# Numerators of two query pairs and transposed rows of the last pair copied to SBUF by ScalarE, and split from there with GpSimd

## The chip, the cores and the metric

One core of a Trainium2 chip runs the whole kernel. The metric is the device time of one execution in microseconds (us). The kernel before takes 561.29 us, the median of 3 runs (561.02 to 561.9).

## What is computed

Two linear-attention blocks work on the same rows x (2048 rows of 576), with 32 heads of 18, and a gate mixes their results row by row. Cut to what matters here:

```python
g = _sigmoid((x * gate_w).sum(-1, keepdims=True))
# block a: phi = where(t > 0, t + 1, exp(t)) + 1e-6
# block b: phi = [softmax(t @ w_phi), softmax(-(t @ w_phi))]
kv  = jnp.einsum("bhsd,bhse->bhde", phi(k), v)
z   = phi(k).sum over s
num = jnp.einsum("bhqd,bhde->bhqe", phi(q), kv)
den = jnp.einsum("bhqd,bhd->bhq", phi(q), z)[..., None] + 1e-6
return g * (num_a / den_a) @ wo_a + (1 - g) * (num_b / den_b) @ wo_b
```

## The kernel before, in words

The 2048 rows are 16 tiles of 128, worked in 8 pairs. Three stages follow each other: keys and values of block a, keys and values of block b, then queries and output of both. Matmul operands are kept as two parts that sum to the float32 value: a high part (F32R, a rounded copy) and a low part (value minus high part). Making both is called a split: ScalarE (A in the code, ACT in the profile) copies the value to the high part, and another engine subtracts it from the value.

This change is in the query stage, from about 290 us to the end. Its loop (lines 1285 to 1309) has nine rounds i. In round i, three strands are merged into one program:

- `q_units` (line 1163) projects pair i+1 with a Strassen product (line 500): seven products in three PSUM tiles of name `pq`, called X, Y and Z here. There are two `pq` buffers: X holds one for the whole pair, and Z takes the buffer of Y. So Z's first matmul (`pq<-tail,x`, with the lhs tile x_3670 for pair 2) waits until VectorE (V, DVE) has added Y into `row` (`row<-row,pq`, line 521). X is accumulated four times, and each time ACT first copies what it holds (`row<-pq`).
- `tr_units` (line 1193) transposes pair i on TensorE, one tile of rows after the other: four transposes of block a's normalized queries (`tr<-ident,row`), whose result in PSUM is split into `at` (high by ACT, low by DVE), and eleven of block b's (`tr<-ident,late`), which ACT copies to `uT`.
- `num` and `out_units` (lines 1214 and 1238) finish pair i-1. `num` multiplies `uT` by `kb` (which merges blocks, `tr<-uT,kb` and `bk<-uT,kb`) into two PSUM tiles `tr` and one `bk`. They are split into `vo` (high by ACT, low by DVE, lines 1227 to 1235: 128x512 for each `tr` tile, 128x256 and 64x256 for `bk`). `out_units` multiplies `at` and `vo` by the output weights: 27 matmuls for each half row, as high times high, high times low and low times high.

There are two PSUM buffers of each name (`tr`, `bk`, `pq`). A transposition into `tr` waits until both readers of the tile that was there before are through.

`norm_a` and `norm_b` (lines 1122 and 1142) divide the queries by their denominators, with work on DVE, GpSimd (G, POOL) and ACT: products with `z_a` and `z_b`, sums over heads (`dd`, `den`), reciprocals, and the scaled rows in `row` and `late`. `softmax_exp` (line 676) makes block b's exponentials in `uw`: maxima and minima (`mm`), two subtractions (`uw<-uw,mm`, `uw<-mm,uw`), one exponential on ACT, sums (`ss`).

The order on each engine is not that of the code. Every operation is recorded in a `Plan` (line 146) with a cost, a time by which it is due, and its dependencies; `run` (line 271) lists the operations by a model of the five engines, and `emit` (line 346) writes them in that order. All instructions therefore have line 354. What the model thought of durations matters on the chip only as the order that it fixed: each engine takes its instructions strictly in that order.

`wk` holds a tile `st` of 128x2x576 with one buffer (line 596). Before this change it is used last in the stage before the queries.

Of the kernel before, what the change touches and what calls it, by code (L numbers as in the profile page):

```python
# [12 lines left out]
F32 = mybir.dt.float32  # L13
F32R = mybir.dt.float32r
AF = mybir.ActivationFunctionType
ALU = mybir.AluOpType
AX = mybir.AxisListType

P = 128
S, D, H, DH = 2048, 576, 32, 18  # L20
NT = S // P
# [337 lines left out]
def tile_gated_mix(ctx, tc, xT, wAk, wAv, wBv, wAq, wkT, wqT, phi, woA, woB, out):  # L359
    nc = tc.nc  # L360
    plan = Plan()
    V, A, G, PE, SP = [Engine(plan, k, x) for k, x in (("DVE", nc.vector), ("ACT", nc.scalar), ("POOL", nc.gpsimd),
                                                       ("PE", nc.tensor), ("SP", nc.sync))]
# [3 lines left out]
    wk = Pool(plan, "wk", ctx.enter_context(tc.tile_pool(name="wk", bufs=2)), 2)  # L367
# [4 lines left out]
    def r(ap):  # L372
        return ap.bitcast(F32)
# [4 lines left out]
    def pq_tile():  # L378
        return ps.tile([P, 2, 512], F32, name="pq")

    def tr_tile():
        return ps.tile([P, 512], F32, name="tr")
# [12 lines left out]
    def bank_tile():  # L395
        return ps.tile([P, 512], F32, name="bk")
# [4 lines left out]
    def uw_tile():  # L401
        return wk.tile([P, 2, D], F32, name="uw")
# [7 lines left out]
    def at_tile(shape, dt=F32):  # L410
        return wk.tile([P] + shape, dt, name="at")

    def wide_tile(i, shape, dt=F32):
        return wk.tile([P] + shape, dt, name=("uT", "late")[i], bufs=1)
# [50 lines left out]
    def chunks(ap):  # L465
        return ap.rearrange("p (j n) -> p j n", n=P)

    def split(src, hi, lo, eng):
        A.activation(hi, src, AF.Copy)
        eng.tensor_tensor(lo, src, r(hi), op=ALU.subtract)  # L470
# [44 lines left out]
    def x_fetch(n):  # L515

        x, ts, stored = x_tiles()
        x["dma"] = []
        for t, d in zip((*ts, *stored), (*X_d[n], *S_d[n])):
            SP.dma_start(r(t), d)  # L520
            x["dma"].append(len(plan.ops) - 1)
        return x
# [245 lines left out]
    raw = area[0][:, :1280].rearrange("p (a c) -> p a c", a=2)  # L768
# [301 lines left out]
    def load_out(k, at):  # L1070
        t = op_tile() if k < 4 else tail_tile()
        WOt[k] = t
        plan.first = at
        if k < 3:
            SP.dma_start(r(t).rearrange("p (i s) n -> p i s n", i=2), WO_d[:, 2 * k:2 * k + 2])
        elif k == 3:
            to = r(t).rearrange("p (i s) n -> p i s n", i=2)
            SP.dma_start(to[:126], MA_d[:252].rearrange("(g p) s n -> p g s n", g=2))
            SP.dma_start(to[126:], MA_d[570:574].rearrange("(g p) s n -> p g s n", g=2))
        else:  # L1080
            SP.dma_start(r(t[:126]), MA_d[252:378])
            SP.dma_start(r(t[126:]), MA_d[574:])
# [80 lines left out]
    def q_units(n, x, uws, c1_tile, then={}):  # L1163
        t1, t2 = 2 * n, 2 * n + 1
        qa, qb = {}, {}

        def c11(c):
            qb[t1] = softmax_exp(c, uws[0], G)

        def c22(c, Z):  # L1170
            V.tensor_tensor(c, c, Z[:, :, :HB], op=ALU.add)
            qa[t2] = phi_elu(c)

        def c21(X):
            qb[t2] = softmax_exp(whole(X, uws[1]), uws[1])

        def c12(c, Z):
            V.tensor_tensor(c, c, Z[:, :, :HB], op=ALU.add)
            qa[t1] = phi_elu(c)

        def norm(t):
            ub = UBS[t % 2]
            qs[t] = (norm_a(t, qa[t], ub), ub)
            norm_b(t, *qb[t], ub, (G, V, G if t < 4 else V))

        x_tile = (two_banks, lambda: two_banks(bank_tile))[n] if n < 2 else pq_tile
        for i, _ in enumerate(strassen(x, WQ, TQ, HB, x_tile, c1_tile, c11, c22, c21, c12)):
            if i in then:
                then[i]()
            yield  # L1190
        norms.extend([lambda: norm(t2), lambda: norm(t1)])

    def tr_units(t, at, uT):
        f, ub = qs.pop(t)
        ath, atl = at
        c = slice(P * (t % 2), P * (t % 2) + P)

        p1 = tr_tile()
        for j in range(4):
            lo = P * j if j < 3 else 448  # L1200
            PE.transpose(p1[:, P * j:P * j + P], f[:, lo:lo + P], ident)
        src = chunks(p1)
        A.activation(ath[:, 0:4, c], src, AF.Copy)
        V.tensor_tensor(atl[:, 0:4, c], src, r(ath[:, 0:4, c]), op=ALU.subtract)
        yield
        for q in range(3):
            p1 = tr_tile()
            nb = min(4, NB - 4 * q)
            for i in range(nb):
                PE.transpose(p1[:UB, P * i:P * i + P], ub[:, UB * (4 * q + i):UB * (4 * q + i) + UB], ident)  # L1210
            A.activation(uT[:UB, 4 * q:4 * q + nb, c], p1[:UB, :P * nb].rearrange("p (j n) -> p j n", n=P), AF.Copy)
            yield

    def num(uT, at, last):
        ath, atl = at
        oh, ol = ot = [wk.tile([P, KT, 256], F32R, name="vo") for _ in range(2)]
        if last:
            q = pq_tile()
            pms = [q[:, 0], q[:, 1], tr_tile()]
        else:  # L1220
            pms = [tr_tile(), tr_tile(), bank_tile()]
        with plan.piece():
            for b in range(NB):
                a, k = b % 2, b // 2 % 2
                PE.matmul(pms[b // 4][64 * a:64 * a + 64, 256 * k:256 * k + 256], kb[:, b, :], uT[:UB, b, :], start=True, stop=True,
                          skip_group_check=True)
        for m, p1 in enumerate(pms):
            j = 2 * m
            n = 2 if j < 4 else 1
            src = p1[:, :256 * n].rearrange("p (j n) -> p j n", n=256)  # L1230
            A.activation(oh[:, j:j + n], src, AF.Copy)
            V.tensor_tensor(ol[:, j:j + n], src, r(oh[:, j:j + n]), op=ALU.subtract)
            if n == 1:
                A.activation(ath[:64, 3], p1[:64, 256:], AF.Copy)
                V.tensor_tensor(atl[:64, 3], p1[:64, 256:], r(ath[:64, 3]), op=ALU.subtract)
        return ot

    def out_units(t, blk):
        ath, atl = blk["at"]
        oh, ol = blk["ot"]  # L1240
        c = slice(P * (t % 2), P * (t % 2) + P)
        osb = row_tile()[:, :D]
        dst = out[P * at_row(t):P * at_row(t) + P]
        for hf in range(2):
            po = bank_tile()
            cc = slice(HB * hf, HB * hf + HB)
            srcs = [(ath, atl, m, 6 + m) for m in range(3)] + [(oh, ol, j, j) for j in range(KT)] + [(ath, atl, 3, 5)]
            st = []
            for hi, lo, j, i in srcs:
                st += [(hi[:, j, c], WO(0, i)), (hi[:, j, c], WO(1, i)), (lo[:, j, c], WO(0, i))]  # L1250
            for i, (l, w) in enumerate(st):
                PE.matmul(po[:, :HB], l, w[:, cc], start=(i == 0), stop=(i == len(st) - 1))
            A.activation(osb[:, cc], po[:, :HB], AF.Copy)
            if t >= NT - 2:
                SP.dma_start(dst[:, cc], osb[:, cc])
            if hf == 0:
                yield
        if t < NT - 2:
            SP.dma_start(dst, osb)
        yield  # L1260
# [10 lines left out]
    def chain(*gens):  # L1271
        for g in gens:
            yield from g
# [3 lines left out]
    uT = wide_tile(0, [NB, 256])  # L1277
# [7 lines left out]
    for i in range(NT // 2 + 1):  # L1285
        while norms:
            norms.pop(0)()
        cur, prev = blocks[i], blocks[i - 1]
        seqs = []
        if i and i <= NT // 2:  # L1290
            prev["ot"] = num(uT, prev["at"], i >= NT // 2 - 1)
        if i + 1 < NT // 2:
            x = x_fetch(pairs[i + 1])
            if i == 0:
                load_out(3, x["dma"])
                load_out(4, x["dma"])
            if i == 1:
                for k, m in enumerate((1, 4, 6)):
                    load_out(k, x["dma"][m:m + 1])
            uws = [extra_uw if i == 0 else uw_tile(), uw_tile()]  # L1300
            seqs.append((7, .7, q_units(i + 1, x, uws, row_tile)))
        ts = (2 * i + 1, 2 * i)
        if i < NT // 2:
            at = at_tile([2, 4, 256], F32R)
            cur["at"] = (at[:, 0], at[:, 1])
            seqs.append((8, 1, chain(*[tr_units(t, cur["at"], uT) for t in ts])))
        if i:
            seqs.append((4, 1, chain(*[out_units(t, prev) for t in (2 * i - 1, 2 * i - 2)])))
        merge(*seqs)
# [82 lines left out]
```

## Time and profile before

| | us |
|---|---|
| median of 3 runs | 561.29 |
| the profiled execution | 562.4 |
| its span, first to last instruction | 560.7 |
| PE (TensorE) busy | 551.6 |
| DVE busy | 421.8 |
| ACT busy | 288.3 |
| POOL busy | 245.8 |

The profile shows one execution. PE is the matmul side of TensorE and PEld its weight loads, which overlap; both are nearly always busy. Times of the timeline count from the span's start. A row of the timeline has the start, the duration, the engine, the operation with out<-in and shapes, how many alike follow each other, and in brackets how long the engine sat idle ahead of it and what ended that. The granted TensorE clock was full for the whole span.

### The profile page before, as it was taken

What the parts mean: (1) busy time and instruction counts of PE and PEld (TensorE: products, weight loads), DVE (VectorE), ACT (ScalarE), POOL (GpSimd) and SP (SyncE); (2) the same over time, 40 slices, a digit from 0 to 9 for tenths busy, and PEclk for the clock granted to TensorE, in tenths of its full rate; (3) what the DMA queues carried; (4) which work ended last, traced back from release to release, by engine and by line L of the source; (5) the groups of instructions that cost most, each with busy time, mean ns of one, the idle gap of its engine ahead of it and who ended that gap; (6) DMA issues with size and microseconds to landing.
All of it is one profiled execution on the core that took longest, in us unless ns stands there. A gap on an engine that the chain in (4) does not pass through costs nothing.

```text
span 560.7 us, 11695 instructions
## 1 busy us (share of the span) xinstructions
PE 551.6 (98%) x4584; PEld 527.7 (94%) x4584; DVE 421.8 (75%) x673; ACT 288.3 (51%) x602; POOL 245.8 (44%) x218
## 2 busy tenths in 40 slices
PE   8999999999999999999999989999999999999997
PEld 8999999999999978999998989898999989899897
DVE  5872678843897997899889998769597795978810
ACT  6666687655645544543355645435443544535421
POOL 6575487632793523363228764214152332424200
PEclk9999999999999999999999999999999999999999
DMA  8739767976759566757759622132322314100001
GB/s 282 272 116 312 252 236 253 338 245 269 273 208 384 184 214 210 250 184 261 284 182 311 247 80 77 48 105 70 106 78 85 97 44 122 51 1 23 31 34 43
DMA packets 38625, 96.22 MB, mean 172 GB/s; under 512 B 4198, under 2 KB 7782, under 8 KB 37034
## 3 DMA queue, kind: packets, MB, share of 16 engines
q1 hardware_dynamic: 38570, 95.47, 50.2%
q8 instruction: 36, 0.59, 0.4%
q14 instruction: 19, 0.16, 0.1%
HBM read 59.64 MB, written 36.70 MB: 172 GB/s over the span
## 4 chain that ended last, share of the span: by engine, by line
PE 83%; DVE 10%; POOL 2%; ACT 2%; issue 1%; DMA 1%; SPq 0%; POOLq 0%; DVEq 0%; ACTq 0%
PE pq L354 35%; PE tr L354 25%; PE bk L354 23%; DVE row L354 3%; DVE dd L354 2%; DVE den L354 1%; DVE mm L354 1%; DVE ss L354 1%; POOL late L354 1%; POOL row L354 1%; DVE at L354 1%; DMA at<-xT 1%; DVE rs L354 1%; ACT row L354 1%; ACT uw L354 0%
## 5 line engine op out<-in xcount | busy, mean ns | idle before, releaser
L354 PE MATMUL pq<-op,x 128*128 128x288 f32 (+1 forms) x636 | 102.6, 297 | 0.0
L354 PEld LDWEIGHTS pq<-op,x 128*128 128x128 f32 x636 | 90.4, 189 | 0.9 <-issue 0.4
L354 PE MATMUL bk<-op,vo 128*128 128x288 f32 x480 | 71.0, 297 | 0.0
L354 PE MATMUL pq<-tail,x 128*128 128x288 f32 (+1 forms) x308 | 66.9, 300 | 0.0
L354 PEld LDWEIGHTS bk<-op,vo 128*128 128x128 f32 x480 | 65.8, 188 | 0.2 <-DVE vo L354 0.2
L354 PE MATMUL pq<-op,xp 128*128 128x288 f32 (+1 forms) x336 | 54.0, 297 | 0.0
L354 PE MATMUL bk<-op,at 128*128 128x288 f32 x288 | 51.3, 301 | 0.0
L354 POOL TENSOR_TENSOR row<-row,z_a 128x576 f32<-128x576 f32 x16 | 22.9, 1429 | 63.3 <-issue 35.7
L354 PEld LDWEIGHTS pq<-tail,x 128*128 128x128 f32 x308 | 49.1, 188 | 1.3 <-issue 0.6
L354 ACT ACTIVATE row<-bk 128x288 f32<-128x288 f32 x38 | 15.6, 411 | 64.4 <-PE bk L354 64.4
L354 PEld LDWEIGHTS pq<-op,xp 128*128 128x128 f32 x336 | 47.5, 188 | 0.2
L354 ACT ACTIVATE row<-row,epsc 128x576 f32<-128x576 f32 x54 | 41.9, 777 | 10.5 <-DVE row L354 9.4
L354 POOL TENSOR_TENSOR row<-row,den 128x378 f32<-128x378 f32 (+1 forms) x32 | 24.6, 789 | 47.8 <-DVE den L354 39.4
L354 DVE TENSOR_REDUCE ss<-uw 128x64 f32<-128x1152 f32 x23 | 31.0, 1350 | 18.5 <-ACT uw L354 17.9
L354 ACT ACTIVATE row<-tr 128x288 f32<-128x288 f32 (+1 forms) x74 | 30.2, 409 | 28.1 <-PE tr L354 27.2
L354 PEld LDWEIGHTS bk<-op,at 128*128 128x128 f32 x288 | 41.7, 189 | 0.4 <-issue 0.4
L354 ACT ACTIVATE uw<-uw 128x1152 f32<-128x1152 f32 x23 | 26.8, 1166 | 23.8 <-DVE uw L354 13.6
L354 POOL TENSOR_TENSOR x<-at,x 128x384 fp32r<-128x384 f32 (+2 forms) x35 | 31.3, 898 | 16.5 <-ACT x L354 14.4
L354 DVE TENSOR_TENSOR row<-row,pq 128x576 f32<-128x576 f32 (+1 forms) x30 | 22.5, 750 | 18.7 <-ACT row L354 14.3
L354 PE MATMUL tr<-op,xv 128*128 128x288 f32 (+1 forms) x204 | 33.7, 302 | 0.0
L354 ACT ACTIVATE uT<-tr 118x512 f32<-118x512 f32 (+1 forms) x48 | 25.9, 559 | 14.6 <-PE tr L354 14.5
L354 DVE TENSOR_TENSOR vo<-row,pq 128x540 f32<-128x540 f32 (+1 forms) x56 | 22.8, 449 | 11.4 <-ACT row L354 10.4
(206 smaller groups left out, 1264.3 us busy)
## 6 DMA issues: line engine op xcount, KB each, us to landing
xp<-s0x SPq DMA_DIRECT2D x12, 512.0 KB
at<-xT SPq DMA_DIRECT2D x18, 320.0 KB
x<-x1x SPq DMA_DIRECT2D x12, 384.0 KB
x<-s2x SPq DMA_DIRECT2D x12, 384.0 KB
s0x<-xp SPq DMA_DIRECT2D x8, 512.0 KB
out<-row SPq DMA_DIRECT2D x14, 288.0 KB
op<-wb SPq DMA_DIRECT2D x3, 1152.0 KB
wod<-op SPq DMA_DIRECT2D x3, 1152.0 KB
```

Source lines behind the costliest of these rows:

```text
L354: fn(*[a.real() if isinstance(a, View) else a for a in args], **{k: v.real() if isinstance(v, View) else v for k, v in kw.items()})
```

## The change

In `num`, for rounds 1 and 2 (the numerators of pairs 0 and 1), each `tr` tile is copied whole to the SBUF tile `st` by ACT. The split then reads `st`: ACT makes the high part from it, and POOL the low part. The `bk` tile is split as before. In `tr_units` the same is done with the four transposes of block a for the last two row tiles (t = 15 and 14, in round 7). Six 128x512 subtractions leave DVE for POOL, and six ACT copies are new.

```diff
@@ tr_units
         src = chunks(p1)
-        A.activation(ath[:, 0:4, c], src, AF.Copy)
-        V.tensor_tensor(atl[:, 0:4, c], src, r(ath[:, 0:4, c]), op=ALU.subtract)
+        if t >= NT - 2:
+            to = chunks(raw_tile()[:, :512])
+            A.activation(to, src, AF.Copy)
+            split(to, ath[:, 0:4, c], atl[:, 0:4, c], G)
+        else:
+            A.activation(ath[:, 0:4, c], src, AF.Copy)
+            V.tensor_tensor(atl[:, 0:4, c], src, r(ath[:, 0:4, c]), op=ALU.subtract)
@@ num
+    def raw_tile():
+        return wk.tile([P, 2, D], F32, name="st", bufs=1).rearrange("p a b -> p (a b)")
+
-    def num(uT, at, last):
+    def num(uT, at, last, raw):
...
+            if raw is not None and n == 2:
+                to = raw[:, 512 * m:512 * m + 512].rearrange("p (j n) -> p j n", n=256)
+                A.activation(to, src, AF.Copy)
+                split(to, oh[:, j:j + n], ol[:, j:j + n], G)
+                continue
@@ the loop
-            prev["ot"] = num(uT, prev["at"], i >= NT // 2 - 1)
+            prev["ot"] = num(uT, prev["at"], i >= NT // 2 - 1, raw_tile() if i in (1, 2) else None)
```

The planner answers with another order of the instructions. It differs in rounds 0 to 2 and from round 7 on; between them each engine has the rows that it had.

The first place is PE in round 1, from the numerators of pair 0 on (`tr<-uT,kb`). The rows `pq<-op,xp` are X and Z of pair 2, and `pq<-tail,x_3670` opens Z. Before:

```order
L354 MATMUL tr<-uT,kb 64x256 x8
L354 MATMUL bk<-uT,kb 64x256 x3
L354 MATMUL pq<-tail,x_3718 128x288
L354 MATMUL pq<-op,xp 128x288 x6
L354 MATMUL bk<-op,vo 128x288 x2
L354 MATMUL pq<-op,xp 128x288 x6
L354 MATMUL pq<-tail,x_3670 128x288 x2
L354 MATMUL pq<-op,xp 128x288 x6
L354 MATMUL pq<-tail,x_3670 128x288 x2
L354 MATMUL pq<-op,xp 128x288 x6
L354 MATMUL pq<-op,x_3895 128x288 x12
L354 MATMUL tr<-ident,row 128x128 x4
```

With the change, PE has at the same place:

```order
L354 MATMUL tr<-uT,kb 64x256 x8
L354 MATMUL bk<-uT,kb 64x256 x3
L354 MATMUL pq<-tail,x_3718 128x288
L354 MATMUL pq<-op,xp 128x288 x6
L354 MATMUL tr<-ident,row 128x128 x4
L354 MATMUL pq<-op,xp 128x288
L354 MATMUL bk<-op,vo 128x288 x2
L354 MATMUL pq<-op,xp 128x288 x5
L354 MATMUL pq<-tail,x_3670 128x288 x2
L354 MATMUL pq<-op,xp 128x288 x6
L354 MATMUL pq<-tail,x_3670 128x288 x2
L354 MATMUL pq<-op,xp 128x288 x6
```

The four transposes have moved up, ahead of Z, and the rest is behind them.

DVE at the same time, before. The row `row<-row,pq` adds Y of pair 2, which Z waits for; `uw` are block b's subtractions for pair 1:

```order
L354 TENSOR_TENSOR row<-vo,z_b 128x576
L354 TENSOR_REDUCE dd<-row 128x32
L354 TENSOR_TENSOR row<-row,pq 128x576
L354 TENSOR_TENSOR dd<-dd,rs 128x64
L354 SCALAR_TENSOR_TENSOR den<-dd 128x32
L354 RECIPROCAL den<-den 128x32
L354 SCALAR_TENSOR_TENSOR rs<-den,gate,rs 128x64
L354 TENSOR_TENSOR uw<-mm,uw 128x576
L354 TENSOR_TENSOR at<-bk,at 64x256
L354 TENSOR_REDUCE mm<-row 128x32 x2
L354 TENSOR_TENSOR uw<-uw,mm 128x576
L354 TENSOR_TENSOR vo<-tr,vo 128x512 x2
```

And with the change:

```order
L354 TENSOR_TENSOR row<-vo,z_b 128x576
L354 TENSOR_REDUCE dd<-row 128x32
L354 TENSOR_REDUCE mm<-uw 128x32
L354 TENSOR_TENSOR uw<-mm,uw 128x576
L354 TENSOR_REDUCE dd<-row 128x32
L354 TENSOR_TENSOR dd<-dd,rs 128x64
L354 SCALAR_TENSOR_TENSOR den<-dd 128x32
L354 RECIPROCAL den<-den 128x32
L354 SCALAR_TENSOR_TENSOR rs<-den,gate,rs 128x64
L354 TENSOR_TENSOR uw<-uw,mm 128x576
L354 TENSOR_TENSOR row<-row,pq 128x576
L354 TENSOR_TENSOR at<-bk,at 64x256
```

The addition of Y has moved behind both `uw` subtractions and the chain from `dd` to `rs`, and the two `vo<-tr,vo` are gone. POOL takes them in this order after the change: `late<-vo,rs` three times, `vo<-st,vo`, `row<-uw,z_b`, `vo<-st,vo`.

The second place is ACT in round 1, late, around the exponential of pair 2 (`uw<-uw`). Before:

```order
L354 ACTIVATE at<-tr 128x4x128
L354 ACTIVATE row<-bk 128x288
L354 ACTIVATE uw<-uw 128x1152
L354 ACTIVATE row<-row 128x3x2
L354 ACTIVATE late<-row 128x10x10
L354 ACTIVATE late<-row 128x46
L354 ACTIVATE uT<-tr 118x4x128 x2
L354 ACTIVATE row<-row,epsc 128x576 x2
```

With the change:

```order
L354 ACTIVATE at<-tr 128x4x128
L354 ACTIVATE row<-bk 128x288
L354 ACTIVATE uT<-tr 118x4x128 x2
L354 ACTIVATE row<-row 128x3x2
L354 ACTIVATE row<-row,epsc 128x576
L354 ACTIVATE uw<-uw 128x1152
L354 ACTIVATE row<-row,epsc 128x576
```

The exponential has moved behind the copies of the next eight transposes (`uT<-tr`).

The third place is PE in round 7, from the numerators of pair 6 on, before:

```order
L354 MATMUL tr<-uT,kb 64x256 x3
L354 MATMUL bk<-op,at 128x288
L354 MATMUL bk<-tail,at 128x288 x3
L354 MATMUL tr<-ident,late 118x128 x3
L354 MATMUL bk<-op,vo 128x288 x2
L354 MATMUL tr<-ident,late 118x128
L354 MATMUL bk<-op,at 128x288 x3
L354 MATMUL bk<-op,vo 128x288 x13
```

With the change:

```order
L354 MATMUL tr<-uT,kb 64x256 x3
L354 MATMUL bk<-op,at 128x288
L354 MATMUL bk<-tail,at 128x288 x3
L354 MATMUL bk<-op,at 128x288 x3
L354 MATMUL bk<-op,vo 128x288 x2
L354 MATMUL tr<-ident,late 118x128 x4
L354 MATMUL bk<-op,vo 128x288 x13
```

The four transposes now stand together, behind two matmuls with the high part of `vo`; the thirteen that follow begin with its low part.

## The prediction

> **What bounds the kernel now.** I read the page's engine totals first, then TensorE's own waits, then the places of those waits in the timeline.
>
> ```profile
> PE 551.6 (98%) x4584; PEld 527.7 (94%) x4584; DVE 421.8 (75%) x673; ACT 288.3 (51%) x602; POOL 245.8 (44%) x218
> ```
>
> TensorE is busy for 551.6 of 560.7 us, and the change leaves its instructions as they are. All that it can win is idle time of TensorE, 9.1 us in all, and it can lose by making new idle time. So I asked who TensorE waits for:
>
> ```profile
> PE tr L354 <- DVE vo L354: 1.8, 2, 1.1
> ...
> PE tr L354 <- POOL late L354: 1.0, 2, 0.6
> PE tr L354 <- DVE at L354: 0.8, 1, 0.8
> ```
>
> Columns: us in total, times, longest. In the query stage these are (timeline of PE):
>
> ```profile
> 326.38 0.66 PE L354 MATMUL tr<-ident,row 128*128 128x128 f32 x4 [1.13 <-DVE vo L354]
> ...
> 335.25 1.09 PE L354 MATMUL tr<-ident,late 128*118 128x128 f32 x8 [0.33 <-POOL late L354]
> ...
> 353.97 0.63 PE L354 MATMUL tr<-ident,row 128*128 128x128 f32 x4 [0.67 <-DVE vo L354]
> 523.78 0.54 PE L354 MATMUL tr<-ident,late 128*118 128x128 f32 x3 [0.82 <-DVE at L354]
> ```
>
> Three of the four are transposes that wait for a `tr` buffer until DVE has taken the low part out of it: 1.13, 0.67 and 0.82 us, at exactly the three places that the change edits. Everywhere else in the stage TensorE is full. Why the first two occur where they do is seen in the windows (sums of busy time by engine; columns PE, PEld, DVE, ACT, POOL):
>
> ```profile
> 320.00:330.00 10.00, 8.87 (x68) 8.60 (x67) 9.66 (x18) 4.99 (x11) 7.65 (x8) 1.00 0.39 118
> ...
> 390.00:400.00 10.00, 10.00 (x78) 10.00 (x78) 6.74 (x14) 3.72 (x8) 3.90 (x4) 1.00 0.27 70
> ```
>
> In the first pairs DVE is the busy one (9.66 of 10) and POOL has 7.65; later DVE has room (6.74) and the same buffers come free in time.
>
> **The change, part by part.** What one split costs, by engine (busy us, mean ns of one):
>
> ```profile
> L354 ACT ACTIVATE vo<-tr 128x512 fp32r<-128x512 f32 x12 | 7.0, 595 | 9.3 <-PE tr L354 9.3
> L354 ACT ACTIVATE xp<-at 128x512 fp32r<-128x512 f32 x8 | 5.0, 631 | 5.7 <-PE pq L354 4.8 <-issue 0.9
> L354 DVE TENSOR_TENSOR vo<-tr,vo 128x512 fp32r<-128x512 f32 x12 | 7.6, 677 | 0.2 <-POOL late L354 0.2
> L354 POOL TENSOR_TENSOR xp<-at,xp 128x512 fp32r<-128x512 f32 x8 | 11.9, 1489 | 5.9 <-PE tr L354 3.3 <-ACT xp L354 2.6
> ```
>
> Six times, ACT gets a copy more (about 0.60), DVE loses 0.68 and POOL gains 1.49. ACT's 3.6 us lie in idle time (4.99 busy of 10 in the tightest window), and the buffer is free after one ACT copy. So the three waits fall, 1.13 + 0.67 + 0.82 us, and I also drop the 0.33 for POOL, since TensorE will arrive there later (below): **2.95 us removed.** The six copies' tile `st` has no other reader left, and the last pair's second copy comes a whole row tile after the first. No DMA is moved past another on SP's queue; the tiles that are loaded have the same users.
>
> **What is late next: Z of pair 2.** The new order puts the addition of Y behind more work on DVE, and Z needs Y's buffer. DVE in the trace of before:
>
> ```profile
> 319.51 0.75 DVE L354 TENSOR_REDUCE dd<-row 128x32 f32<-128x576 f32 x1
> 320.18 0.74 DVE L354 TENSOR_TENSOR row<-row,pq 128x576 f32<-128x576 f32 x1
> 320.83 0.22 DVE L354 TENSOR_TENSOR dd<-dd,rs 128x64 f32<-128x64 f32 x1
> 321.09 0.19 DVE L354 SCALAR_TENSOR_TENSOR den<-dd 128x32 f32<-128x32 f32 x1
> 321.31 0.35 DVE L354 RECIPROCAL den<-den 128x32 f32<-128x32 f32 x1
> 321.70 0.28 DVE L354 SCALAR_TENSOR_TENSOR rs<-den,gate,rs 128x64 f32<-128x64 f32 x1
> 321.91 0.75 DVE L354 TENSOR_TENSOR uw<-mm,uw 128x576 f32<-128x576 f32 x1
> ...
> 324.23 1.20 DVE L354 TENSOR_TENSOR uw<-uw,mm 128x576 f32<-128x576 f32 x1
> ```
>
> Up to here the new order has the same DVE work, less one `dd` (0.67 from start to start), so its `uw<-mm,uw` gets its turn at about 319.5. Then come `uw<-mm,uw` 0.67, `dd` 0.67, the chain to `rs` 1.08 (320.83 to 321.91), `uw<-uw,mm` 0.67 and the addition 0.74: it ends at 323.3 if nothing holds it. TensorE comes to Z much sooner:
>
> ```profile
> 319.51 0.96 PE L354 MATMUL pq<-op,xp 128*128 128x288 f32 x6
> 320.31 0.43 PE L354 MATMUL bk<-op,vo 128*128 128x288 f32 x2
> 320.57 0.96 PE L354 MATMUL pq<-op,xp 128*128 128x288 f32 x6
> 321.37 0.42 PE L354 MATMUL pq<-tail,x 128*128 128x288 f32 x2
> ```
>
> Z began at 321.37; with four transposes ahead of it (0.45) it is due at 321.8. The wait is at least 1.5 us. TensorE takes its list in order, so all of Z, X and the outputs queue behind it. And something does hold DVE:
>
> ```profile
> 313.74 0.76 DVE L354 SCALAR_TENSOR_TENSOR row<-row 128x576 f32<-128x576 f32 x1 [0.15 <-ACT row L354]
> 313.77 2.02 POOL L354 TENSOR_TENSOR row<-vo,z_b 128x576 f32<-128x576 f32 x1
> ...
> 318.94 1.70 POOL L354 TENSOR_TENSOR row<-row,den 128x378 f32<-128x378 f32 x2 [0.50 <-DVE den L354]
> 322.16 3.44 POOL L354 TENSOR_TENSOR late<-vo,rs 128x540 f32<-128x540 f32 x3 [1.52 <-DVE rs L354]
> ...
> 342.26 2.81 POOL L354 TENSOR_TENSOR row<-uw,z_b 128x576 f32<-128x576 f32 x2 [0.77 <-ACT uw L354]
> 344.14 1.53 DVE L354 TENSOR_TENSOR row<-uw,z_b 128x576 f32<-128x576 f32 x1
> ```
>
> At 344.14 DVE starts in the middle of POOL's second product (it ends at 345.07), takes 1.53 instead of 0.75, and ends 0.60 after POOL does: it stood still until POOL was through. At 313.77 it is the reverse: POOL takes 2.02 instead of 1.4. Products of two SBUF operands on both engines take turns, whole instructions at a time; the PSUM subtractions beside POOL stay at 0.68. In the new order POOL's `row<-vo,z_b` (1.4) follows its first `row<-row,den` (0.8), which gives way to DVE's `row<-vo,z_b`; so it runs from about 319.2 to 320.65, just when `uw<-mm,uw` is due at 319.5. That is 1.15 more, and Z waits 2.7. If `uw<-uw,mm` meets `late<-vo,rs` as it did at 324.23 (1.20 instead of 0.75), 3.1. I take **2.7, bounds 1.5 and 3.1**; the 2.7 is nearest to how the rows above behave.
>
> [...]
>
> **POOL's low parts.** They come after `late<-vo,rs` (from 323.8, 2.6), so at 326.4 + 1.3 to 1.5, and TensorE is due for them at 324.5 + 16 + 6 matmuls of 0.133 = 327.4: a wait of 0.3 to 0.5. The second has `row<-uw,z_b` (1.4) and perhaps one turn of DVE (0.7) ahead of it: 0 to 0.5. I take **0.6, bounds 0 and 1.0**.
>
> **Pair 1's round.** The exponential of pair 2 now stands behind the next `uT` copies.
>
> ```profile
> 341.02 1.16 ACT L354 ACTIVATE uw<-uw 128x1152 f32<-128x1152 f32 x1
> ...
> 358.96 0.60 PE L354 MATMUL tr<-ident,late 128*118 128x128 f32 x4
> ...
> 359.77 0.75 DVE L354 TENSOR_TENSOR row<-row,pq 128x576 f32<-128x576 f32 x1
> ```
>
> It moves by some 4 us on that clock, to 345.2, after two `uT` copies and a Relu. The DVE work from its sums to the next addition of Y, 21 instructions of the new order at the durations that such rows have here (0.2 to 1.35), is about 13 us, so that one ends near 359.6 or, with three or four turns of POOL in between, near 362; Z of pair 3, less the wait that fell, is due at 360.7. I take **0.5, bounds 0 and 1.4.**
>
> **The last pair.** The transposes no longer wait, but the low part of `vo` follows two `late` products and a `den` sum on DVE:
>
> ```profile
> 521.65 1.48 DVE L354 TENSOR_TENSOR late<-uw,rs 128x540 f32<-128x540 f32 x2
> 524.30 1.28 DVE L354 TENSOR_TENSOR vo<-pq,vo 128x512 fp32r<-128x512 f32 x2
> ...
> 525.04 2.00 PE L354 MATMUL bk<-op,vo 128*128 128x288 f32 x13
> ```
>
> It is done at 521.65 + 1.48 + 0.67 + 0.68 = 524.5, or 0.3 later if POOL's new subtraction holds a `late` product. The thirteen matmuls began at 525.04, so of the 0.82 only 0.2 to 0.6 comes back: **0.45 added, bounds 0.25 and 0.6.**
>
> Sum: -2.95 + 2.7 + 0.6 + 0.5 + 0.45 = **+1.3 us**. All lower bounds give -1.2, all upper ones +3.15. The profiled execution took 562.4 us (1.7 around its span), 1.1 above the median shown; against it the sum is 563.7, against the median 562.6. I forecast the median. A measurement of this kernel can tell about 0.2% (1.1 us) from no change.
>
> **Rivals.**
> - Faster: DVE runs ahead of the old times, since 1.35 us of subtractions in the busiest stretch are gone and POOL never meets it at 319.5. Z then waits 1.5 or less and the low parts are in time: -1.2, so 560.1; if the addition of Y ended before 321.8, the point from which this decides, all three waits would go for nothing: 558.7. For it: the waits sit exactly where the change edits. Against: 323.3 needs no collision at all, and is still too late.
> - No change that can be told: the collision costs half, Z waits 2.0, and pair 3's Z nothing: near 561.3. For it: removed and added terms are of one size.
> - Slower by more: the turns add up, DVE stays late into pair 3 and every upper bound holds: 564.4. For it: DVE's 9.66 of 10 leaves no room to catch up before pair 2. Against: from 360 on it has room.
> - The change doesn't free the buffer sooner, because ACT copies late: then the waits stay and the added terms come on top, also near 564. ACT's half-idle windows speak against it; I count it into the case before.
>
> **How the numbers follow.** The forecast (562.4 to 563.4) has 0.36, slower by more 0.09, no change 0.33, faster 0.22. The predicted time is the first one's. The range of 8 in 10 runs from 559.6, which takes in 560.1 and leaves out the end of the faster case, to 564.2, just under all upper bounds. Slower has 0.36 + 0.09 = 0.45.
>
> **What would show it.** Right: no PE wait for DVE `vo` at the four transposes of rounds 1 and 2; instead one of 2 to 3 us ahead of `pq<-tail,x` near 322, ended by DVE `row`; `uw<-mm,uw` of DVE longer than 1 us near 320; short PE waits for POOL `vo`; near 524 a wait for DVE `vo` in place of DVE `at`. Wrong: Z starting near 322 with no wait, or DVE's `uw` products at 0.75 beside POOL's.

## The result

| | before | after |
|---|---|---|
| time, median of 21 runs each | 561.40 us (560.63 to 563.38) | 562.32 us (561.55 to 563.97) |
| ratio, 95% interval | | 1.0015 [1.0008, 1.0022] |
| profiled execution: time, span | 562.4, 560.7 | 561.81, 560.1 |

The change makes the kernel slower by 0.92 us, or 0.15%. Forecast was +1.3, as 562.6. The number is close, but further down it shows that it is so for two reasons that cancel each other in part.

The page of the changed kernel, its line of totals by engine (busy us, share of the span, instructions):

```profile
PE 551.0 (98%) x4584; PEld 526.9 (94%) x4584; DVE 420.4 (75%) x667; ACT 291.2 (52%) x608; POOL 254.8 (45%) x224
```

ACT has 2.9 us more, POOL 9.0 more, and TensorE's work is the same. DVE has only 1.4 less, although six subtractions of 0.68 have left it: some of its other products now take longer beside POOL (examples stand further down). As before, all is decided by who TensorE waits for (us in total, times, longest):

```profile
PE pq L354 <- DVE row L354: 2.2, 2, 2.0
...
PE tr L354 <- DVE late L354: 0.7, 1, 0.7
PE tr L354 <- POOL late L354: 0.6, 1, 0.6
...
PE tr L354 <- DVE vo L354: 0.2, 1, 0.2
```

The 1.8 for DVE `vo` at the places of the change and the 0.8 for DVE `at` are gone; 2.2 for DVE `row` and 0.7 for DVE `late` have come. Their places, in TensorE's timeline (start, us, operation, and in brackets the idle time before with what ended it):

```profile
319.43 0.60 PE L354 MATMUL tr<-ident,row 128*128 128x128 f32 x4
...
323.06 0.54 PE L354 MATMUL pq<-tail,x 128*128 128x288 f32 x2 [1.97 <-DVE row L354]
...
326.19 1.06 PE L354 MATMUL bk<-op,vo 128*128 128x288 f32 x6
...
334.73 1.09 PE L354 MATMUL tr<-ident,late 128*118 128x128 f32 x8
...
352.33 0.60 PE L354 MATMUL tr<-ident,row 128*128 128x128 f32 x4
...
360.77 0.53 PE L354 MATMUL pq<-tail,x 128*128 128x288 f32 x2 [0.19 <-DVE row L354]
...
523.94 0.62 PE L354 MATMUL tr<-ident,late 128*118 128x128 f32 x4 [0.68 <-DVE late L354]
```

The transposes of rounds 1 and 2 and the `late` ones at 334.73 have no bracket any more: these waits fell. Z of pair 2 has one of 1.97, pair 3's Z one of 0.19, and the last pair one of 0.68. The 0.2 left for DVE `vo` is new too: 0.19 ahead of four transposes at 387.76, in round 3, whose order the change leaves as it was.

**Where to measure.** Up to some 300 us both programs are the same, and up to the numerators of round 1 only a few instructions change places. Yet this first part took 0.9 us less in the execution shown here. One reason lies in the start. In the trace of before, TensorE starts its matmuls of the projections 0.24 us apart up to the first record of a full clock, at 11.94 us, and 0.13 apart from there; in after that record stands at 8.81. So the clock was not full for the whole span, as is said with the profile of before. In the first 20 us TensorE has 100 matmuls in before, 111 in after, which has the shortest first part of all profiled executions, 104 to 106 in e1 to e3 and 86 in e4, which has the longest. The end of the first part is the start of the products with `kb`; first the row of before, then that of after:

```profile
316.54 1.95 PE L354 MATMUL tr<-uT,kb 118*64 118x256 f32 x16
```

```profile
315.64 1.95 PE L354 MATMUL tr<-uT,kb 118*64 118x256 f32 x16
```

From there to the end of the span (560.70 and 560.09 to two places): 560.70 - 316.54 = 244.16 before and 560.09 - 315.64 = 244.45 after, **+0.3**. I call this the rest below. It is a sharper measure than the whole time, since the first part ended anywhere between 315.64 and 318.48 in twelve profiled executions, of kernels that hardly differ there; the six with the order of before alone spread over 0.8. It leaves 0.6 of the 0.92 open: does the profiled execution lack something that other executions have? It does. Each run also lists TensorE's mean granted clock:

| kernel | runs at 0.996 or 0.997 | runs at 0.999 or 1.0 |
|---|---|---|
| before, beside the experiments | 0 | 69 |
| after | 12, median 562.70 us | 9, median 561.97 us |

The profiled execution of after was one of the nine.

### The profile page after: what moved, and what is told of

Read it like the earlier page. It is cut to its first block, busy times and chain, and to the rows that moved or that the text cites. A ratio compares the mean times of both kernels' runs of the same rounds, so it can differ in the third digit from the quotient of the medians.

```text
span 560.1 us, 11710 instructions
## 1 busy us (share of the span) xinstructions
PE 551.0 (98%) x4584; PEld 526.9 (94%) x4584; DVE 420.4 (75%) x667; ACT 291.2 (52%) x608; POOL 254.8 (45%) x224
```

## The experiments

All were timed against the kernel before on the same chip. Before had medians of 561.95 us beside e1 to e4, 561.56 beside e5 to e8 and 561.69 beside e9 and e10. "Rest" is the span less the start of that first `tr<-uT,kb`; before has 244.16. In the expectations, "the numerators of pair 1" and "of pair 2" are those of rounds 1 and 2, which the description above counts as pairs 0 and 1; below I go by rounds.

| run | median us | ratio [95%] | rest, us | runs at low clock | longest new wait of TensorE |
|---|---|---|---|---|---|
| after | 562.32 | 1.0015 [1.0008, 1.0022] | 244.45 | 12 of 21 | 1.97 |
| e1 round 1 alone | 562.74 | 1.0011 [1.0002, 1.0021] | 245.06 | 10 of 12 | 1.98 |
| e2 round 2 alone | 562.26 | 1.0006 [0.9997, 1.0014] | 244.50 | 0 of 12 | 0.93 |
| e3 last pair alone | 561.70 | 0.9995 [0.9986, 1.0003] | 243.98 | 0 of 11 | 0.68 |
| e4 Y first | 563.70 | 1.0033 [1.0019, 1.0048] | 245.84 | 10 of 11 | 2.37 |
| e5 wait filled | 561.81 | 1.0005 [0.9997, 1.0014] | 244.47 | 0 of 11 | 0.67 |
| e6 delay of 3 | 563.96 | 1.0041 [1.0027, 1.0055] | 246.16 | 2 of 6 | 1.73 |
| e7 delay of 2 | 563.25 | 1.0030 [1.0020, 1.0040] | 245.34 | 0 of 8 | 1.00 |
| e8 other order | 561.04 | 0.9983 [0.9974, 0.9992] | 243.29 | 0 of 11 | 1.34 |
| e9 other order, mended | 557.98 | 0.9932 [0.9919, 0.9946] | 240.93 | 0 of 5 | 0.61 |
| e10 its round 2 and last pair alone | 559.93 | 0.9968 [0.9956, 0.9981] | 242.10 | 0 of 5 | none |

### e1, e2, e3: one part of the change at a time

```diff
e1, e2 (tr_units)
-        if t >= NT - 2:
+        if False:
e1 (the call of num)
-raw_tile() if i in (1, 2) else None
+raw_tile() if i == 1 else None
e2
-raw_tile() if i in (1, 2) else None
+raw_tile() if i == 2 else None
e3
-raw_tile() if i in (1, 2) else None
+None
```

> Only the numerators of pair 1 go through the copy and POOL; pair 2 and the last pair stay as before. Theory A (the forecast's: the new order around pair 1 puts the addition of Y behind other DVE work): TensorE's waits of 1.13 (DVE vo, near 326) and 0.33 (POOL late, near 335) go, one of about 2.0 for DVE row comes ahead of Z near 322 and about 0.4 ahead of pair 3's Z: +0.9 us, 562.3. Theory B (each extra copy and each POOL subtraction costs by itself, wherever it stands): a third of the whole difference, +0.3 us, 561.7. Theory C (the gain of 1.13 is real and the difference seen is not of this stage): -1.1, 560.3.

> Only the numerators of pair 2 go through the copy and POOL. Theory A: the wait of 0.67 for DVE vo near 354 goes and nothing takes its place, since DVE has room there and the order moves little: -0.6 us, 560.8. Theory B: +0.3, 561.7, with the 0.67 gone but POOL's subtractions holding DVE's products. If a wait for POOL vo appears near 354 to 357 instead, no change: 561.4.

> Only the last pair's transposed rows go through the copy and POOL. Theory A by the trace of the changed kernel: the wait of 0.82 for DVE at is replaced by one of 0.68 for DVE late: -0.1 us, 561.3. By the forecast's own step (0.82 gone, 0.45 back as a wait for DVE vo): -0.4, 561.0. Theory B: +0.3, 561.7.

By medians against before the three are worth +0.79, +0.31 and -0.25, in sum +0.85, and the whole change +0.92. The intervals are some 0.5 us to either side, and only e1's leaves out no change; so within that noise the parts add up, and the largest is round 1. Theory B foretold +0.3 for each part. e3's interval ends at +0.17, so copies and POOL subtractions have no price of their own that shows there, and e2's +0.31 has another reason, shown below. In e1 TensorE waits ahead of Z as in after (timeline of TensorE):

```profile
323.35 0.53 PE L354 MATMUL pq<-tail,x 128*128 128x288 f32 x2 [1.98 <-DVE row L354]
323.72 0.95 PE L354 MATMUL pq<-op,xp 128*128 128x288 f32 x6
...
324.79 1.64 PE L354 MATMUL pq<-op,xp 128*128 128x288 f32 x6
```

Two equal groups of six, the second 0.69 longer, with no wait between. The reason stands in the windows of the same execution; the number behind ACT's and POOL's busy times is the granted clock:

```profile
324.00:324.50 0.50, 0.50 (x6) 0.50 (x5) 0.50 (x2) 0.50 (x2) 0.50 (x1) 1.00 0.00 0
324.50:325.00 0.50, 0.50 (x5) 0.50 (x4) 0.50 (x1) 0.50 (x3) 0.50 (x2) 0.73 0.00 0
325.00:325.50 0.50, 0.50 (x3) 0.50 (x3) 0.50 (x1) 0.25 (x2) 0.42 (x2) 0.50 0.00 0
...
328.00:328.50 0.50, 0.50 (x5) 0.50 (x5) 0.50 (x2) 0.00 (x0) 0.50 (x1) 0.86 0.82 279
328.50:329.00 0.50, 0.50 (x6) 0.50 (x5) 0.50 (x1) 0.00 (x0) 0.50 (x1) 1.00 0.98 401
```

From 324.73 (0.73 is the mean of 1.00 for 0.23 us and 0.50 for 0.27) to 328.14 the clock is 0.50, for 3.4 us, 1.4 us after a wait of two. From the `kb` products of round 1 to those of round 2, e1 needs 34.01 us and after, with the same order there and full clock, 32.93: the low clock costs 1.08. It could be 3.4 x 0.5 = 1.7 at most. Without it e1's rest would be 245.06 - 1.08 = 243.98, 0.2 below before: by this, all that e1 loses is the low clock. Two waits differ from its expectation. Pair 3's Z doesn't wait, and the 0.67 of round 2 is gone as well, although round 2 is not copied there: DVE's `vo<-tr,vo` stands ahead of the `late` products in e1's order and behind them in that of before.

In e2, alone, the wait didn't go but changed hands. TensorE, then POOL:

```profile
355.36 1.06 PE L354 MATMUL bk<-op,vo 128*128 128x288 f32 x6 [0.93 <-POOL vo L354]
```

```profile
352.87 1.22 POOL L354 TENSOR_TENSOR row<-row,den 128x378 f32<-128x378 f32 x1 [4.08 <-DVE den L354]
354.05 2.51 POOL L354 TENSOR_TENSOR vo<-st,vo 128x512 fp32r<-128x512 f32 x2
```

POOL takes its list in order; the subtractions stand behind a product that waits 4.08 us for DVE. That is the last case of its expectation, and 0.93 in place of 0.67 fits the +0.3 in the rest. In e3 the wait is as in after, 0.68 for DVE `late`, in place of 0.82.

### e4: Y first

What stands on DVE in round 1, before the edit (-) and after it (+):

```diff
 mm<-uw
-uw<-mm,uw
-dd<-row
-dd<-dd,rs
-den<-dd
-den<-den
-rs<-den,gate,rs
-uw<-uw,mm
 row<-row,pq
+dd<-row
+dd<-dd,rs
+den<-dd
+den<-den
+rs<-den,gate,rs
+uw<-mm,uw
+uw<-uw,mm
 at<-bk,at
```

> The changed kernel with the same instructions in another order at one place: on DVE the addition of Y of pair 2 stands ahead of dd, the chain to rs, uw<-mm,uw and uw<-uw,mm, and on ACT the copies at<-tr and row<-pq ahead of the exponential. Theory A, simple form: the wait of 1.97 ahead of Z goes and the rest stays: 560.4, 1.9 below the changed kernel. Theory A2: the wait ahead of Z covers another one. The first low part of vo lands on POOL at 326.1 in the changed kernel, and TensorE, 1.97 us earlier, would want it at 324.2: a wait of 1.5 to 2 us for POOL vo takes its place, 561.9 to 562.3. Theory B: no change against the changed kernel, 562.3, but without a wait for POOL vo.

Theory A2 holds, its simple form falls: the wait for Y is gone, and this is in its place.

```profile
329.22 1.81 PE L424 MATMUL bk<-op,vo 128*128 128x288 f32 x6 [2.37 <-POOL vo L424]
```

So the 1.97 for Y in after covered a wait for POOL's low part that would have come anyway. The chain behind it is one that I had on paper only as "they come after `late<-vo,rs`": the low part is written into a buffer that the tile `extra_uw` (exponentials of pair 1, under the name `vo`) still holds, and the last that reads it is POOL's `late<-vo,rs`. The time, 563.70, is above the changed kernel's, where I had expected 562.3 at most, and the clock shows why:

```profile
329.00:329.50 0.50, 0.28 (x1) 0.28 (x2) 0.47 (x2) 0.00 (x0) 0.50 (x2) 0.62 0.01 0
329.50:330.00 0.50, 0.50 (x3) 0.50 (x4) 0.50 (x3) 0.00 (x0) 0.50 (x1) 0.50 0.00 0
...
332.00:332.50 0.50, 0.50 (x3) 0.50 (x3) 0.50 (x2) 0.00 (x0) 0.50 (x1) 0.50 0.00 0
332.50:333.00 0.50, 0.50 (x5) 0.50 (x5) 0.50 (x2) 0.00 (x0) 0.50 (x1) 0.97 0.00 0
```

Again 0.50 for 3.4 us (329.12 to 332.53), and 10 of 11 runs have the low mean clock. From here on theory D was the question: a long wait costs twice.

### e5: the same wait, filled with work

```diff
+        at = order.index(self.ops[3195])
+        order[at:at] = self.ops[3114:3118] * 5
         with tc.manual_schedule():
```

> The changed kernel, with the four transposes of round 1 (tr<-ident,row) done five times more, directly ahead of Z of pair 2: twenty extra instructions of TensorE that give the same result again and fill its wait of 1.97 for DVE row. Theory D (the wait costs twice: its own length, and in most executions a stretch of some 3.4 us at a granted clock of 0.5 behind it, which TensorE gets for having been idle): Z starts when it did, the mean granted clock is 0.999 to 1.0 in all runs instead of 0.996 to 0.997 in 12 of 21, and the median is 562.0, that of the changed kernel's runs at full clock. Rival (the low clock is chance, or comes from the POOL or ACT work at that place): the clock stays at 0.996 to 0.997 in more than half of the runs, and the time at 562.3 or above.

```profile
321.44 2.35 PE L356 MATMUL tr<-ident,row 128*128 128x128 f32 x20
323.59 0.54 PE L356 MATMUL pq<-tail,x 128*128 128x288 f32 x2
```

The twenty transposes fill the wait, Z isn't sooner (the rest is 244.47, after has 244.45), and none of 11 runs has the low clock, where 12 of 21 had it. The median falls to 561.81. So the low clock goes with TensorE's being idle, not with what POOL or ACT do there, and at full clock the change costs +0.25 us against before, an interval that takes in no change.

### e6, e7: the wait alone, elsewhere

```diff
+        at = order.index(self.ops[4170])
+        order[at:at] = [self.ops[4088]] * 3
         with tc.manual_schedule():
```

(e7: `* 2`.) `ops[4170]` is the addition of Y of a later pair, `ops[4088]` the `late` product ahead of it.

> The kernel before, with one product of DVE (late<-uw,rs, 0.67 from start to start) done three times more ahead of the addition of Y of one later pair, near 428, where nothing of the change is. Z of that pair was in time to 0.2 us, so TensorE waits about 1.9 there. Theory D: the mean clock is 0.996 to 0.997 in more than half of the runs and the time 1.9 + 1.0 above the kernel before: 564.5 in those, 563.6 in the others. Rival (the wait costs its length and no more): clock 0.999 to 1.0, 563.6 in all. If DVE's delay runs on into the next waits, both are later by some tenths.

> As the run before with two repeats in place of three: TensorE waits about 1.2 near 428, as long as the waits that the kernel before has near 326. Theory D with a limit between 1.3 and 2.0 us: the clock stays at 0.999 to 1.0 and the time is 1.2 above the kernel before, 562.9. If the limit is lower than that, some runs show 0.997 and 563.7.

First e6, then e7:

```profile
430.77 0.53 PE L356 MATMUL pq<-tail,x 128*128 128x288 f32 x2 [1.73 <-DVE row L356]
```

```profile
429.97 0.54 PE L356 MATMUL pq<-tail,x 128*128 128x288 f32 x2 [1.00 <-DVE row L356]
```

The waits came out some 0.2 shorter than planned. With 1.73, two of six runs have the low clock, and their median is 564.97 against 563.54 for the other four; with 1.00, none of eight. The rests, at full clock, are 2.0 and 1.2 above before. e7's median is 0.35 above the 562.9 expected. That is Theory D in kind, at a place where nothing of the change is; that "more than half" of e6's runs would show it was wrong, and with six runs the share is rough. The profiled execution of e6 is one of the four at full clock, so the waits of the other two were not seen.

### e8, e9, e10: is there a version that beats both?

In e8 nothing goes to another engine. DVE's order, and one tile's name:

```diff
-    extra_uw = wk.tile([P, 2, D], F32, name="vo")
+    extra_uw = wk.tile([P, 2, D], F32, name="st", bufs=1)
round 1
 uw<-mm,uw
+uw<-uw,mm
+vo<-tr,vo x2
 at<-bk,at
 mm<-row x2
-uw<-uw,mm
-vo<-tr,vo x2
round 2
 rs<-den,gate,rs
+vo<-tr,vo
 late<-uw,rs x3
...
-vo<-tr,vo x2
+vo<-tr,vo
last pair
 dd<-row x2
-row<-row
 dd<-dd,rs
...
-dd<-row
 rs<-den,gate,rs
 late<-uw,rs x2
 at<-tr,at
-den<-row
+row<-row
+dd<-row
 vo<-pq,vo x2
+den<-row
```

> The kernel before, no work moved to another engine: the tile extra_uw takes the tile st, which is free then, so that the low parts of vo of pair 1 need not wait for POOL's late<-vo,rs, and on DVE alone the order is another at the three places: pair 1 uw<-uw,mm and the two vo<-tr,vo ahead of at<-bk,at and the two mm; pair 2 the first vo<-tr,vo ahead of the late products; last pair the sums and the chain to rs, the late products and at<-tr,at ahead of the Relu product, the dd and the den sum. Theory A (the three waits are only DVE's order and one buffer): 1.13 + 0.67 + 0.82 us go and nothing comes instead: 558.8 to 559.3. Rival (DVE is full in the first pairs, whatever goes first makes something else late): the waits at pairs 1 and 2 turn into others of the same size, and only the last pair's 0.8 is gained: 560.7.

TensorE's waits in e8:

```profile
PE tr L423 <- POOL late L423: 1.9, 2, 1.3
PE bk L423 <- DVE vo L423: 1.3, 1, 1.3
```

The rival was right at round 1 and wrong at round 2. Round 2's 0.67 and the last pair's 0.82 are gone; at round 1, the third low part came too late (1.34) and the chain to POOL's `late` as well (1.31 in place of 0.33). e9 takes these two out, e10 leaves round 1 as before:

```diff
e9, DVE
 uw<-mm,uw
 uw<-uw,mm
 vo<-tr,vo x2
+vo<-bk,vo
 at<-bk,at
-mm<-row x2
 ss<-uw
 rs<-ss
-vo<-bk,vo
 at<-tr,at
...
 row<-row,pq
-ss<-uw
-rs<-ss
+mm<-row x2
...
 uw<-pq,mm
+ss<-uw
+rs<-ss
e9, POOL
-uw<-mm,row
-uw<-row,mm
 row<-uw,z_b
 late<-uw,rs x3
 row<-row,z_a
+uw<-mm,row
+uw<-row,mm
e9, ACT
-uw<-uw
 row<-bk
...
 at<-tr
+uw<-uw
```

> The run e8 with its two new waits taken out: at pair 1 the third low part, vo<-bk,vo, and at<-bk,at follow the two vo<-tr,vo at once on DVE, and the two mm with all that hangs on them (POOL's uw<-mm,row and uw<-row,mm, ACT's exponential, ss and rs) go behind the chain that feeds POOL's late<-uw,rs. Theory A: all of 1.13 + 0.67 + 0.82 goes and the wait for POOL late stays at 0.3 to 0.6: 558.8 to 559.3, and 1.5 to 2 below e8. Rival (DVE is full in that round): a wait of about 1 us comes elsewhere between 330 and 350, 560.3.

> The kernel before with the DVE order of e8 at pair 2 and the last pair alone; pair 1 and the tile of extra_uw as before. Theory A: 0.67 + 0.82 goes, the 1.13 near 326 and the 0.33 near 335 stay: 1.5 below the kernel before, 560.0. If pair 2 or the last pair takes its gain back further on, 560.7 to 561.

First e9's one wait that is left in round 1, then e10's two:

```profile
334.25 1.09 PE L423 MATMUL tr<-ident,late 128*118 128x128 f32 x8 [0.61 <-POOL late L423]
```

```profile
325.90 0.66 PE L423 MATMUL tr<-ident,row 128*128 128x128 f32 x4 [1.13 <-DVE vo L423]
...
334.78 1.09 PE L423 MATMUL tr<-ident,late 128*118 128x128 f32 x8 [0.32 <-POOL late L423]
```

e10 took 559.93, as expected (560.0). **e9 took 557.98 us, 0.68% less than before**, with every wait that the change aimed at gone and nothing of its size in their place. It is about 1 us better than I expected; in the rest, the gain is 3.2 against 2.3 of listed waits (1.13 + 0.67 + 0.82 - 0.28). At the last pair, from the products with `kb` to the end takes 1.3 less for a listed wait of 0.82, so the idle time in the brackets isn't all that such a place loses. Within the rest, TensorE's busy time is also lower, 237.08 against 237.88, for the same matmuls. The four transposes that stand behind a wait at 326.38 in before took 0.66, those with no wait ahead at 319.43 in after 0.60. So idle time, which the prediction took for all that can be won, is not all; why such a group takes longer stays open.

## Why the prediction was right, and where it was wrong

**The four waits, -2.95: right.** None of the four is in the changed kernel. But the reason was only half seen. At round 1 the copy lets `tr` go while the low part goes on waiting for a buffer. At round 2 the order that comes with round 1's part is enough, since the 0.67 is gone in e1 without a copy there; the copy of round 2 alone (e2) only put 0.93 in its place.

**Z of pair 2, +2.7: right in kind, 1.97 in size.** DVE and POOL of after, in the timeline; the profile's clock is 0.9 earlier than in before:

```profile
318.48 1.34 DVE L354 TENSOR_TENSOR uw<-mm,uw 128x576 f32<-128x576 f32 x1
...
321.60 0.75 DVE L354 TENSOR_TENSOR uw<-uw,mm 128x576 f32<-128x576 f32 x1
322.26 0.75 DVE L354 TENSOR_TENSOR row<-row,pq 128x576 f32<-128x576 f32 x1
```

```profile
317.76 1.44 POOL L354 TENSOR_TENSOR row<-vo,z_b 128x576 f32<-128x576 f32 x1
...
321.85 2.92 POOL L354 TENSOR_TENSOR late<-vo,rs 128x540 f32<-128x540 f32 x3 [1.65 <-DVE rs L354]
324.84 1.30 POOL L354 TENSOR_TENSOR vo<-st,vo 128x512 fp32r<-128x512 f32 x1
```

DVE's product of two SBUF operands stands still until POOL is through at 319.20, as predicted. But POOL began 0.5 earlier than I had reckoned, so it cost 0.6 (1.34 against 0.75) and not 1.15. The second one, `uw<-uw,mm`, began 0.25 ahead of POOL's `late<-vo,rs` and took its usual 0.75; there it was POOL that took longer, 2.92 for the three against 2.57 for `late<-uw,rs` at 332.37. So in both places the products took turns, as the rows in the prediction did. What I mis-sized is how long DVE stands still.

**POOL's low parts, +0.6: nothing.** The first ends at 324.84 + 1.30 = 326.14, and TensorE comes for it at 326.19. It is late only if Z isn't (e4: 2.37). The two terms hang on one chain and can't be added.

**Pair 3's Z, +0.5: 0.19.** Another 0.19 for DVE `vo` comes at 387.76, which the prediction didn't have.

**The last pair, +0.45 as a wait for DVE `vo`: 0.68 as one for DVE `late`.** The step failed in what the new order does. POOL, then DVE:

```profile
520.38 1.28 POOL L354 TENSOR_TENSOR at<-st,at 128x512 fp32r<-128x512 f32 x1 [0.39 <-ACT at L354]
```

```profile
520.96 0.78 DVE L354 SCALAR_TENSOR_TENSOR rs<-den,gate,rs 128x64 f32<-128x64 f32 x1
521.78 0.72 DVE L354 TENSOR_TENSOR late<-uw,rs 128x540 f32<-128x540 f32 x1
522.42 0.74 DVE L354 TENSOR_REDUCE den<-row 128x32 f32<-128x576 f32 x1
523.08 0.71 DVE L354 TENSOR_TENSOR late<-uw,rs 128x540 f32<-128x540 f32 x1
```

The new subtraction holds even a small `rs` (0.78 against 0.27 before), as the two of round 2 do with a small `dd` and `den` (1.25 and 1.17 at 351.50 and 352.79, against 0.70 and 0.19 before), and a sum now stands between the two `late` products; the transposes need both. I had seen both possibilities, and priced neither at TensorE's transposes.

**The sum.** The listed waits come to -2.95 + 1.97 + 0.19 + 0.19 + 0.68 = +0.1, and the rest measured +0.3, the difference being busy time of TensorE (238.16 against 237.88); predicted was +1.3. To this the clock adds what 12 of 21 runs show: as a rough estimate 12/21 x 1.08 = 0.6, so 0.9 in all, where 0.92 was measured. That it fits so closely is luck: the nine runs at full clock alone have a median 0.57 above before, and e5 has 0.25. That the low clock of these twelve runs lies behind Z is concluded from e1 (same order, seen there) and from e5 (filled, gone); no execution of after with a low clock was profiled.

**The step that failed** is therefore the price of a wait: "Z of pair 2 waits 2.7" was put into the sum at its length, like the waits of 1.13, 0.67 and 0.82 that it replaces. A wait of two us isn't three of 0.67. I traded three short waits for one long one, and the long one has a second price, the low clock (1.08 in e1's trace). That term (0.6) was left out and the others came out 1.0 too high, so the two errors cancelled in part, and how close the number came is luck. What held is the direction and the main wait: Z of pair 2, ended by DVE `row`. The measured +0.15%, whose interval leaves out no change, lies within the 0.2% that I had called too small to tell. That case had 0.33, with the conditions "the collision costs half, Z waits 2.0, and pair 3's Z nothing", which is almost what the trace shows.

Of what was to show it, three came (no wait for DVE `vo` at the four transposes, one of 1.97 for DVE `row` ahead of Z, just under the 2 to 3 named, and `uw<-mm,uw` over 1 us) and two didn't (short waits for POOL `vo`, and DVE `vo` near 524). One sign of being wrong came as well, a `uw` product at 0.75 beside POOL's; it had started first.

## What to carry to other kernels

Don't add waits up as if they were all alike: several short ones may be cheaper than one long one of the same sum (here the low clock came with a wait of 1.97 or 1.98 in 22 of 33 runs, with 1.34 or less in none of 42), so look at the granted clock of all runs, not of the profiled one alone. Where an engine's buffer comes free late, ask what the writer of the next tile waits for before moving work to another engine; here one tile's place and the order on three engines gave 3.7 us by medians (3.2 in the rest), where the move to ACT and POOL lost 0.9. And measure a late stage from the last point that both programs have in common.

## What was not expected of the hardware

After TensorE had been idle for about two us, its granted clock went to 0.50 for 3.41 us: in e1 from 324.73 to 328.14, which begins 1.38 after the end of a wait of 1.98, and in e4 from 329.12 to 332.53, which begins 0.10 before the end of one of 2.37. It came in some executions of a kernel and not in others. By the longest new wait of the profiled execution, the mean clock is 0.996 or 0.997 in 22 of 33 runs with 1.97 or 1.98 (after, e1), in 10 of 11 with 2.37 (e4), in 2 of 6 with 1.73 (e6), in none of 42 with 1.34 or less (e2, e3, e7, e8), and never in 69 runs of before. It costs 0.7 to 1.4 us (after 562.70 against 561.97, e6 564.97 against 563.54; e1's trace 1.08). With twenty transposes that compute nothing new in place of the wait, none of 11 runs has it (e5).

What decides in which executions the clock falls is not shown. The profiled execution of after kept full clock with a wait of 1.97, and that of e6 with one of 1.73; e1's lost it with 1.98. The length of the wait alone doesn't tell them apart, so for waits of this size the share has to be counted over many runs.
